# A planner's landing time, 1.9 to 4.0: one constant in the list scheduler of a three-stage kernel

## The chip, the cores and the metric

The kernel runs on one core of one Trainium2 chip. The metric is device time in microseconds of one launch. Engines are named as in the profile: PE (TensorE), DVE (VectorE), ACT (ScalarE), POOL (GpSimd) and SP (SyncE, which issues every transfer here).

## The reference

```python
# attention (b=4, h=8, s=576, d=64): softmax of q over d, of k over the sequence
kv = np.einsum('bhsd,bhse->bhde', softmax_s(k), v)
x = np.einsum('bhsd,bhde->bhse', softmax_d(q), kv)        # then x as 2304 x 512
# first block: w_in 512 x 2048, w_out 2048 x 512
h = x @ w_in
x = (h * np.clip(h + 3.0, 0.0, 6.0) / 6.0) @ w_out
# second block: 4 experts, w1 512 x 1024, w2 1024 x 512, p = domain_probs normalised per token
out = sum(p[:, e:e+1] * (np.maximum(x @ w1[e], 0.0) @ w2[e]) for e in range(4))
```

## The kernel before

**Work and stages.** A prologue turns q and k of the four batches into the first block's input `x0` (`k_part`, `q_part`, `x_part`). A first stage computes the first block, 16 chunks of 128 hidden columns over six token blocks of 384 (`h_part`: products on L638 to L640, then L682). Its weights come in 64-bit form and are rebuilt word by word on DVE, ACT and POOL (`w_part`: load L576, then L586 to L608). Meanwhile other weights for the end are prepared and stored to DRAM (`w_prepare`: ACT L831, POOL, store L837 into `vd`). Then come three units of 768 tokens of the second block. Unit 0 prepares its weights as it goes and stores some (`w_first0`, `w_second0`: load L872, ACT L897 and L931, store L903; PE L1094 and L1216). Units 1 and 2 load what was stored (`w_bring`, L864; PE L973 and L1289). Every value is split in a high and a low part, and three matmuls make one product. POOL's and some of DVE's element-wise work goes through one helper, L347.

**The order of the work.** No engine's order is written by hand. Each piece of work is an `Op` with a cost on each engine that may do it, its dependencies, the buffer it takes and the buffers it gives back. `Plan.order()` runs a model of the core in time: on each engine, when its clock is free, it takes the op with the smallest key among those whose inputs have arrived and whose buffer is free. The ops are then emitted in the order of their modelled starts, so each engine's queue holds that order and runs it first come, first served, waiting on semaphores for what really happens. The modelled times are used for nothing else. The model starts SP at 2.0 (`FIRST`) and the engines at 5.6 (`BEGIN`).

A transfer costs its KB divided by 400 on SP, one after the other (`dma(n)`, 0.64 for 256 KB, 0.72 for 288 KB, 1.28 for 512 KB). What depends on it arrives `LAND` after that:

```python
def hop(a, b):
    return LAND if a == "SP" else HOPS[b]
...
    # in Plan.order():
    o.due = min((x.due - self.after(e, x) for x in o.then), default=1e6) - o.eng[e].lat
...
    for kind, name in o.give:                       # a buffer given back by o
        self.free[kind].append([..., o.end + hop(e, "")])
    for x in o.then:
        x.at = max(x.at, o.end + self.after(e, x))  # when x may start
```

From SP to SP `after` gives 0. An op's key is its due time (worked back from the PE products in their fixed turn) plus a small bias; the first stage's own DVE and ACT work has keys near -10000, so it always goes first; output stores have key 0. PE's products of each stage are chained, so their order among themselves is fixed. Only one kind of buffer is given back by a transfer: the tiles `wr` of `w_prepare`, free once the store L837 has landed (two of them at first, four from a late part of the first stage on).

Of the kernel before, what the change touches and what calls it, by code (L numbers as in the profile page):

```python
# [76 lines left out]


HOPS = {"PE": 0.06, "ACT": 0.05, "DVE": 0.05, "Pool": 0.09, "SP": 0.05, "": 0.0}
LAND = 1.9  # L80


class Cost(float):
# [9 lines left out]
def hop(a, b):  # L93
    return LAND if a == "SP" else HOPS[b]

# [1439 lines left out]
```

## Time and profile before

| what | value |
|---|---|
| median of 3 runs | 1235.85 us (1231.95 to 1236.56) |
| the profiled execution | 1234.68 us, span 1232.9 us |
| PE busy | 1197.6 us (97%), 7296 matmuls |
| DVE, ACT, POOL busy | 779.1, 600.7, 757.7 us |
| mean granted TensorE clock | 0.994 of full speed |
| DMA | 238.99 MB, mean 194 GB/s |
| chain that ended last | PE 80%, POOL 6%, DMA 5%, DVE 4% |

PE's busy time is that of the matmuls as the profile models them. Times in rows are counted from the start of the span. "Issue to landing" is from SP's issue of a transfer to the moment at which its semaphore says that it has landed.

### The profile page before, as it was taken

The page shows a single profiled execution, that of the slowest core. Times are in us where ns is not written, and L with a number is a line of the kernel's source. Part 1 is how long each engine was busy: PE and PEld are TensorE (multiplying, and loading weights), DVE is VectorE, ACT ScalarE, POOL GpSimd, SP SyncE. Part 2 cuts the span into 40 slices and gives each one's busy share as a digit, 9 for nine tenths or more (in the row PEclk, how much of TensorE's full clock was granted, in tenths as well). Part 3 has the DMA queues.
Part 4 walks back from the last instruction along what each step waited for, and adds up shares of the span by engine and source line. Part 5 has one row for each costly group of instructions (what it writes and reads, how often), then busy time and mean ns, then how long its engine had stood idle before and what let it go on. Part 6 is the DMA issues. An engine that isn't in the chain of part 4 may idle for free.

```text
span 1232.9 us, 21178 instructions
## 1 busy us (share of the span) xinstructions
PE 1197.6 (97%) x7296; PEld 1146.5 (93%) x7296; DVE 779.1 (63%) x1362; ACT 600.7 (49%) x1256; POOL 757.7 (61%) x780
## 2 busy tenths in 40 slices
PE   5699999999999999999999999999999999999998
PEld 4589999999999999988988889999999999999998
DVE  6877731668763555555555575666666966666665
ACT  6667544645554543644444444444444544444441
POOL 4677677766688630877777705655555565555552
PEclk9899999999999999999999999999999999999999
DMA  9533444244367430565555547877777787777771
GB/s 318 154 95 104 162 162 164 103 145 147 135 222 256 152 131 1 178 214 180 182 182 190 183 159 232 275 248 250 249 248 250 241 294 250 247 247 249 246 249 59
DMA packets 125275, 238.99 MB, mean 194 GB/s; under 512 B 14064, under 2 KB 14064, under 8 KB 125168
## 3 DMA queue, kind: packets, MB, share of 16 engines
q1 hardware_dynamic: 125168, 237.64, 57.9%
q8 instruction: 58, 0.95, 0.3%
q14 instruction: 49, 0.40, 0.1%
HBM read 174.14 MB, written 63.44 MB: 193 GB/s over the span
## 4 chain that ended last, share of the span: by engine, by line
PE 80%; POOL 6%; DMA 5%; DVE 4%; issue 3%; ACT 1%; SPq 0%; DVEq 0%; POOLq 0%; ACTq 0%
PE ps L1289 19%; PE ps L973 19%; PE ps L1216 11%; PE ps L1094 9%; PE ps L682 9%; POOL w L347 3%; PE ps L638 3%; PE ps L640 3%; PE ps L639 3%; DMA vd<-w 3%; POOL st L347 1%; DMA qs<-in_q_dram 1%; PE ps L437 1%; POOL wtmp L347 1%; PE ps L531 1%
## 5 line engine op out<-in xcount | busy, mean ns | idle before, releaser
L973 PE MATMUL ps<-x,w 128*128 128x384 f32 x1344 | 264.4, 335 | 0.0
L1289 PE MATMUL ps<-w,g 128*128 128x256 f32 x1737 | 244.0, 283 | 1.7 <-DVE acc L1338 1.7
L347 POOL TENSOR_TENSOR w<-st,w 128x256 fp32r<-128x256 f32 (+1 forms) x174 | 173.8, 1016 | 114.7 <-ACT w L931 76.8
L1289 PEld LDWEIGHTS ps<-w,g 128*128 128x128 f32 x1737 | 228.6, 189 | 5.0 <-DVE acc L1338 5.0
L682 PE MATMUL ps<-g,w 128*128 128x384 f32 x1152 | 223.2, 339 | 5.0 <-ACT g L661 4.1
L973 PEld LDWEIGHTS ps<-x,w 128*128 128x128 f32 x1344 | 227.2, 189 | 0.8
L347 POOL TENSOR_TENSOR g<-t,g 128x384 fp32r<-128x384 f32 x128 | 140.9, 1109 | 124.8 <-ACT g L996 108.4
L682 PEld LDWEIGHTS ps<-g,w 128*128 128x128 f32 x1152 | 199.4, 188 | 12.4 <-ACT g L661 7.6
L1338 DVE SCALAR_TENSOR_TENSOR acc<-ps,pt,acc 128x256 f32<-128x256 f32 x312 | 144.2, 480 | 99.2 <-PE ps L1289 97.6
L1216 PE MATMUL ps<-w,g 128*128 128x512 f32 x576 | 148.9, 394 | 0.0
L1094 PE MATMUL ps<-x,w 128*128 128x384 f32 x672 | 131.0, 335 | 0.0
L655 DVE SCALAR_TENSOR_TENSOR r<-r,ps 128x384 f32<-128x384 f32 x96 | 53.0, 552 | 122.1 <-ACT r L652 114.4
L638 PE MATMUL ps<-x,w 128*128 128x384 f32 x384 | 129.0, 336 | 0.0
L640 PE MATMUL ps<-x,w 128*128 128x384 f32 x384 | 128.5, 335 | 0.3 <-POOL w L347 0.3
L639 PE MATMUL ps<-x,w 128*128 128x384 f32 x384 | 128.3, 334 | 0.0
L1094 PEld LDWEIGHTS ps<-x,w 128*128 128x128 f32 x672 | 119.4, 188 | 7.8
L1216 PEld LDWEIGHTS ps<-w,g 128*128 128x128 f32 x576 | 106.6, 188 | 16.7
L347 POOL TENSOR_TENSOR st<-st 128x256 f32<-128x256 f32 (+1 forms) x66 | 74.4, 1131 | 48.6 <-DVE st L601 45.3
L996 ACT ACTIVATE g<-t 128x384 fp32r<-128x384 f32 x143 | 74.6, 525 | 59.3 <-DVE t L1038 21.6
L652 ACT ACTIVATE r<-ps,three 128x384 f32<-128x384 f32 x96 | 55.4, 577 | 76.1 <-PE ps L640 75.0
L347 POOL TENSOR_TENSOR t<-t 128x384 f32<-128x384 f32 x47 | 47.9, 1020 | 45.3 <-ACT t L981 38.9
L981 ACT ACTIVATE t<-ps 128x384 f32<-128x384 f32 x104 | 50.3, 484 | 52.1 <-PE ps L973 51.5
(145 smaller groups left out, 1852.4 us busy)
## 6 DMA issues: line engine op xcount, KB each, us to landing
w<-wd SPq DMA_DIRECT2D x224, 256.0 KB, 3.1
w<-vd SPq DMA_DIRECT2D x224, 256.0 KB, 3.6
vd<-w SPq DMA_DIRECT2D x112, 256.0 KB, 2.2
wd<-w SPq DMA_DIRECT2D x112, 256.0 KB, 3.5
st<-in_w_dram SPq DMA_DIRECT2D x64, 256.0 KB, 3.5
st<-in_w_dram SPq DMA_DIRECT2D x30, 512.0 KB, 3.9
raw<-in_w_dram SPq DMA_DIRECT2D x32, 256.0 KB, 3.7
out_dram<-acc SPq DMA_DIRECT2D x18, 256.0 KB, 2.5
```

The costliest lines, as they stand in the source:

```text
L347: on(o).tensor_tensor(out=out, in0=a, in1=b, op=op)
L638: nc.tensor.matmul(pst[0], lhsT=hi, rhs=a, start=(k == 0), stop=False)
L639: nc.tensor.matmul(pst[0], lhsT=hi, rhs=b, start=False, stop=False)
L640: nc.tensor.matmul(pst[0], lhsT=lo, rhs=a, start=False, stop=(k == NK - 1))
L652: nc.scalar.activation(out=pst["r"], in_=pst[0], func=AF.Relu, bias=three)
L682: nc.tensor.matmul(y, lhsT=l, rhs=r, start=(s["start"] and not low and m == 0), stop=(s["stop"] and bool(low)))
L973: nc.tensor.matmul(bank(i), lhsT=l, rhs=r, start=(opens and k == 0 and m == 0), stop=(k == 1 and m == 2), skip_group_check=not opens)
L996: nc.scalar.activation(out=made[i][0][:, :n], in_=at(src), func=AF.Relu if raw else AF.Copy)
L1094: nc.tensor.matmul(bank(i), lhsT=l, rhs=r, start=(opens and k == 0 and m == 0), stop=(k == 1 and m == 2), skip_group_check=not opens)
L1216: nc.tensor.matmul(y, lhsT=l, rhs=rr, start=opens and x == 0, stop=closes and x == len(seq) - 1)
L1289: nc.tensor.matmul(y, lhsT=l, rhs=r, start=clears and x == 0, stop=x == len(seq) - 1, skip_group_check=True)
L1338: o1 = add({"DVE": dvep(half)}, lambda o: nc.vector.scalar_tensor_tensor(out=a, in0=y, scalar=s, in1=a, op0=ALU.mult, op1=ALU.add), [made])
```

## The change

The model's time from the end of a transfer's stream to its landing goes from 1.9 to 4.0. Nothing that computes is touched. The constant enters three things: when an op that needs a loaded tile may start in the model, when a `wr` tile is free again after its store, and the due time of each transfer and of all that leads to it.

```diff
 HOPS = {"PE": 0.06, "ACT": 0.05, "DVE": 0.05, "Pool": 0.09, "SP": 0.05, "": 0.0}
-LAND = 1.9
+LAND = 4.0
```

## Rows read from the trace of the kernel before

**Rows 1.** Stretch, length, each engine's busy us (instructions), granted clock, DMA share, GB/s.
```profile
0.00:100.00 100.00, 75.97 (x435) 62.54 (x436) 76.26 (x173) 68.00 (x149) 62.96 (x63) 0.93 0.57 184
...
240.00:420.00 180.00, 174.61 (x979) 168.37 (x979) 116.83 (x190) 95.41 (x200) 131.16 (x141) 1.00 0.52 177
...
500.00:980.00 480.00, 480.00 (x2853) 453.56 (x2852) 305.54 (x494) 226.15 (x477) 300.52 (x310) 1.00 0.66 218
980.00:1200.00 220.00, 218.82 (x1546) 217.20 (x1546) 152.32 (x278) 94.79 (x194) 128.43 (x120) 1.00 0.79 254
```

**Rows 2.** PE's waits in 240 to 420: for whom, us, times, longest.
```profile
PE ps L682 <- ACT g L661: 4.1, 7, 1.5
PE ps L640 <- POOL w L347: 0.3, 1, 0.3
```

**Rows 3.** Transfers in the first 26 us: KB each, median us to landing.
```profile
acc<-in_kt_dram SPq DMA_DIRECT2D x6, 288.0 KB, 4.7
...
qs<-in_q_dram SPq DMA_DIRECT2D x6, 256.0 KB, 4.8
```

**Rows 4.** Transfers between 26 and 100 us, the same view.
```profile
st<-in_w_dram SPq DMA_DIRECT2D x5, 512.0 KB, 3.9
acc<-in_kt_dram SPq DMA_DIRECT2D x7, 288.0 KB, 3.1
...
qs<-in_q_dram SPq DMA_DIRECT2D x6, 256.0 KB, 2.9
```

**Rows 5.** Order of time from 0 to 9 us: start, us, instruction, idle before.
```profile
1.19 0.42 SPq L418 DMA_DIRECT2D acc<-in_kt_dram  x1
...
3.38 0.69 DVE L494 TENSOR_REDUCE qm<-qs 128x8 f32<-128x512 f32 x1 [1.96 <-DMA qs<-in_q_dram]
...
5.94 0.69 DVE L494 TENSOR_REDUCE qm<-qs 128x8 f32<-128x512 f32 x1 [1.87 <-DMA qs<-in_q_dram]
6.54 0.74 DVE L449 TENSOR_REDUCE nm<-acc 128x1 f32<-128x576 f32 x1
```

**Rows 6.** The first two transfers: KB, us from issue to landing.
```profile
acc<-in_kt_dram SPq DMA_DIRECT2D x1, 288.0 KB, 3.0
qs<-in_q_dram SPq DMA_DIRECT2D x1, 256.0 KB, 2.6
```

**Rows 7.** Order of time from 26.8 to 32 us, DVE and PE.
```profile
26.92 1.38 PE L437 MATMUL ps<-vs,acc 128*128 128x129 f32 x10 [0.38 <-DVE acc L344]
...
28.79 0.69 DVE L494 TENSOR_REDUCE qm<-qs 128x8 f32<-128x512 f32 x1 [1.92 <-DMA qs<-in_q_dram]
...
30.59 0.16 DVE L444 RECIPROCAL rs<-ps 128x1 f32<-128x1 f32 x1
...
31.29 1.09 PE L430 MATMUL ps<-ident,acc 128*128 128x128 f32 x4 [2.98 <-DVE bd L445]
```

**Rows 8.** The chain that ended last, its piece from 21 to 29 us.
```profile
21.12 7.57 DMA qs<-in_q_dram
```

**Rows 9.** The stretch with the lowest clock, columns as in Rows 1.
```profile
30.00:35.00 5.00, 3.34 (x14) 2.77 (x15) 4.09 (x11) 2.27 (x7) 3.99 (x4) 0.50 0.37 116
```

**Rows 10.** DVE's waits for transfers in the first 120 us: us, times, longest.
```profile
DVE qm L494 <- DMA qs<-in_q_dram: 9.3, 7, 2.0
...
DVE qm L494 <- DMA spare<-in_q_dram: 1.8, 1, 1.8
```

**Rows 11.** SP's longest wait in the first 120 us, the same columns.
```profile
SPq L420 <- PE ps L437: 26.1, 8, 10.1
```

**Rows 12.** ACT's waits in 200 to 420 us, the longest in total.
```profile
ACT w L831 <- DMA vd<-w: 36.2, 35, 4.1
```

**Rows 13.** The stores of line 837 between 140 and 220 us.
```profile
L837 SPq DMA_DIRECT2D vd<-w x37: 319/320/399, 142.1 to 218.8; - x37
...
DMA to landing us min/median/max: 2.0/2.0/3.9
```

**Rows 14.** POOL's longest wait between 400 and 520 us.
```profile
POOL w L347 <- ACT w L931: 52.8, 2, 51.2
```

## The prediction

> **What bounds the kernel now.** I read first the busy time by stretch. From 500 to 980 us PE is busy in all 480 us, and from 980 to 1200 in 218.8 of 220; between 240 and 420 it loses 5.4 us, and in the first 100 us it loses 24.0 [rows 1]. So the kernel is bound by PE's fixed sequence of matmuls, and an order that a planner makes can move only what PE loses: 24.0 in the prologue, 5.4 in the middle of the first stage, little more behind. Next, who PE waited for: in the middle it is mostly ACT (4.1 of the 5.4), and nowhere in that list a transfer [rows 2]. In the prologue DVE is busy 76.3 of 100 us and leads PE [rows 1], and DVE does wait for transfers, 9.3 and 1.8 us [rows 10]. So a landing time matters here through DVE's and ACT's queues, which run in the order that the plan gave them and stand still at an op whose load has not landed.
>
> The constant is a guess about landings, so the third view is what they really take. In the plan a 256 KB load asked for on an idle queue lands 0.64 + 1.9 = 2.54 after its issue, and with the change 4.64; for 288 KB it is 2.62 and 4.72, for 512 KB 3.18 and 5.28. On the chip these loads took 4.8 and 4.7 us while everything was loading at once [rows 3], and 2.9, 3.1 and 3.9 us afterwards [rows 4]. So in the first 26 us 4.0 is the better guess (some of that time is queueing, which the plan counts separately). Behind that both are wrong: 1.9 is 0.4 to 0.7 too early, 4.0 is 1.4 to 1.7 too late.
>
> **Three things that cannot change.** The constant adds no instruction and no byte. PE's products keep their order within a stage, as they are chained. Due times move, but those of all plain loads by the same 2.1, so their order on SP among themselves changes only where the time at which a buffer comes free decides. SP stands waiting for such buffers anyway, 26.1 us for one of them alone [rows 11]; a load that is put ahead of another can block it there, and this is why I keep a slower case.
>
> **The change part by part.**
>
> *The opening.* In the plan before, the first q tile arrives at 4.54, the first k tile at 5.26, the second q at 5.90; DVE starts at 5.6, so when it has reduced the first q (0.6) both others are there and the smaller key wins: q, q, k. The trace shows that order, and that DVE stood idle for 1.87 us before the second q [rows 5], although the first k, issued at 1.19, had landed 3.0 us later, at 4.19 [rows 5, 6]. With 4.0 the arrivals are 6.64, 7.36 and 8.00. DVE is free of the first q at 7.24, and the k tile comes next: q, k, q. On the chip the k reduction (0.74) then fits into the idle 1.87. I take 0.7 us saved; bounds nothing (DVE's total work is the same, and what follows may wait for something else) and 1.9.
>
> *The gap at 28 us.* PE ends a product at 28.30 and then waits 2.98 us for `bd`, which DVE makes on L444 and L445. DVE could not: it waited 1.92 us for a q tile at the head of its queue, then did three other ops, and reached L444 at 30.59 [rows 7]. That q tile was 7.57 us on its way [rows 8]. If the plan lets it arrive 2.1 later, its reduction falls behind ops that were ready, and L444 can start as early as 28.3: 2.3 us sooner. The idle stretch also has a second price. After it the granted clock was 0.50 for 5 us, in which PE was busy 3.34 us [rows 9]; at full clock that is half, 1.7 less. Together 4.0. Other ops may get in front of L444 in the new order as well, so I take 3.0, bounds 0 and 4.0.
>
> *The later loads of the prologue.* The 16 k tiles go through four buffers, so behind the first generation come three more, each with a landing in its chain. There the plan will expect a tile 1.7 us later than it lands (4.64 against 2.9), and puts other work in front of its first op. If all three generations pay this on the path to PE, it is 5.1; with the full 2.1 each, 6.3; if DVE, which is busy three quarters of the time, had other work to do anyway, nothing. I take the middle, 2.6 lost.
>
> *The first stage, stores.* A `wr` tile is free in the plan at 2.54 after its store's start, and then at 4.64. Really stores landed in 2.0 us between 140 and 220 [rows 13], yet ACT waited 36.2 us for them between 200 and 420, up to 4.1 at a time [rows 12], because the stores started late. With the tile planned free 2.1 later, ACT's op L831 stands further back in its queue, and the op of the main chain behind it is not held up. The main chain's waits for ACT are 4.1 us of PE time [rows 2]. Not all come from L831; I take 1.5 saved, bounds 0 and 4.1.
>
> *The same stores, the other way.* The preparation becomes slower. Two tiles in a ring give one store per half cycle; 37 stores took from 142.1 to 218.8, 2.13 us each [rows 13]. With 2.1 more per cycle it is 1.05 more each, 3.18, so in that stretch 24 are done in place of 37. The 13 missing come at the end, where the ring has four tiles and a cycle in the plan of 4.64 + 1.3 (0.3 on ACT, 0.7 on POOL and the hops, by the plan's costs) for four, 1.5 each: 20 us later. This is hidden by POOL's wait of 51.2 us in 400 to 520, in which all of this work is over and there is no buffer to go on with [rows 14]. Cost nothing; if the delay grew past 51 us, PE would stand for what is above it.
>
> *The first stage, the 64-bit weights.* Their load is planned 2.1 later, and DVE's, ACT's and POOL's steps with it. Really a 512 KB load takes 3.9 [rows 4], so they stand 1.4 too late in their queues. PE waited for such a tile once, 0.3 us [rows 2]; two or three chunks are needed at once where the pass over all six blocks begins. Bounds nothing and 3 x 2.1 = 6.3; I take 1.0 lost.
>
> *Units 0 to 2.* PE never lacked a weight tile in 500 to 980 [rows 1]: nothing.
>
> *Sum.* -0.7 - 3.0 + 2.6 - 1.5 + 1.0 = -1.6. Against the profiled execution's own 1234.68 that is 1233.1. The median of the runs lies 1.2 above the profiled one, so against it I forecast 1234. The bounds added up are -10.0 (1.9 + 4.0 + 4.1) and +12.6 (6.3 + 6.3), 1226 and 1248.
>
> A rule of the Trainium skill speaks against the change: "DMA: Bandwidth & Descriptors", section "Anatomy of one DMA", gives a transfer a fixed part of about 2.0 us beside bytes at 436 GB/s, on another issue path than SP's. For 256 KB that makes 2.6 us, and the first transfer, alone on the queue, did take 2.6 [rows 6]. By the rule 1.9 would be right everywhere, the first and second terms would be empty, and the sum would be +2.1; the landings of 4.7 and 4.8 under load [rows 3] say otherwise for the opening.
>
> **The rivals.**
>
> *Faster.* All of DVE's waits for transfers in the prologue but the first, unavoidable one (9.3 + 1.8 - 1.96 = 9.1 [rows 5, 10]) come off PE's path, and with them the slow clock at 30 us (1.7) [rows 9]: -10.8, 1225. For it speaks that they are the wait that the constant aims at; against it that DVE is busy 76.3 of the 100 us, so much of what is filled in returns as work later. Chance 0.25.
>
> *Slower.* A first op on a landed tile, or a load on SP behind one that waits, comes late on the prologue's path. Three generations at 2.1 are 6.3, and if PE thereby gets one more idle stretch like that at 28 us (2.98 idle and 1.7 of slow clock), it is +11.0: 1247. It decides from the point at which an op on a k or q tile starts more than 2 us after its landing while PE is idle. Against it speaks that in the plan all consumers move alike. Chance 0.24.
>
> *The ring of stores.* The preparation ends more than 51 us later than now, PE stands at the start of unit 0; at twice the 20 us worked out it does not. Were it four times, 80 us, PE would lose 29: 1265. Chance 0.05.
>
> *No effect.* The order changes only among ops that do not lead PE: 1236. This and the forecast fall in the same class, together 0.46 (0.36 for the forecast, 0.10 for this).
>
> **How the numbers follow.** About 0.5%, 6 us, is what a measurement of this kernel can tell from no change. Faster than that 0.25, within it 0.36 + 0.10 = 0.46, slower 0.24 + 0.05 = 0.29. The likeliest time is 1234. The range reaches from the faster rival, 1225, with 3 us more for a second gap closed, to the slower one, 1247, with 4 more for the same reason: 1222 to 1251; the ring and extremes of the others lie outside.
>
> **What would show it.** In the new trace: DVE's second reduction is of a k tile; its waits for q tiles in the first 120 us fall below 11 us; no PE wait of 3 us at 28 us; ACT's wait for stores in 200 to 420 well under 36 us; fewer than 30 stores of L837 between 140 and 220, the last of them some 20 us later than now, POOL's 51 us wait shortened by as much; PE full from 500 on. Wrong would be: the prologue's loss above 30 us, new stretches at a clock of 0.5, PE waiting for POOL or DVE on weight tiles between 220 and 300, or PE idle at the start of unit 0.

## The result, and the profile after

The changed kernel takes 1223.5 us (median of 4 runs, 1222.7 to 1224.9) against 1235.5 before: a ratio of 0.9909, 95% interval 0.9887 to 0.9931. It is faster by 0.9%, 12 us. The time lies in the range that I gave, near its lower end; the likeliest case, no change that can be told, did not come. (The median before is that of four runs; the 1235.85 ahead of the prediction was that of the first three.) The profiled execution has a span of 1223.1 us.

Busy time by stretch, after (the columns of [rows 1]):

```profile
0.00:100.00 100.00, 79.47 (x445) 66.07 (x446) 80.56 (x179) 69.07 (x150) 63.31 (x63) 0.90 0.58 192
...
240.00:420.00 180.00, 178.82 (x1031) 178.38 (x1030) 124.67 (x198) 97.86 (x206) 134.43 (x142) 1.00 0.50 172
...
500.00:980.00 480.00, 478.82 (x2855) 451.76 (x2854) 303.08 (x496) 223.57 (x470) 299.13 (x307) 1.00 0.67 218
980.00:1200.00 220.00, 220.00 (x1555) 218.20 (x1554) 150.18 (x274) 93.47 (x192) 126.55 (x119) 1.00 0.78 248
```

The second busy column is that of PE's weight loads, the figure in brackets their number. Between 240 and 420 it goes from 168.37 (979 loads) to 178.38 (1030): 10 us more of full work in the same 180 us. The first busy column, the matmuls', shows only 4.2 of that (174.61 to 178.82). Behind 500 the weight loads differ by less than 2 us in either stretch.

The start of PE's products on line 638 gives the same account as a clock (four such matmuls belong to one step of the first stage, of which there are 96). Undisturbed, a step takes 4.16 us. Step 12, behind the prologue's thick part, starts at 137.9 us before and 136.6 after; step 36 at 237.7 and 236.5; unit 0's first matmul (L1094) at 500.1 and 489.8; from there to the start of the last matmul it is 728.4 and 728.9. So in these two profiles 1.3 us come from the prologue, 9.1 from the first stage behind step 36, and none from the units. (What the prologue's share is worth in other executions is told below.)

What stood in PE's way in that stretch has gone. PE's weight loads show the wait for ACT in full; between 240 and 420, first before, then after (us, times, longest):

```profile
PEld ps L682 <- ACT g L661: 7.6, 11, 1.8
```

```profile
PEld ps L682 <- ACT g L661: 1.5, 1, 1.5
```

The matmuls' only wait for ACT there, after, in us, times and longest (4.1 in 7 before [rows 2]), and ACT's wait for stores between 200 and 420 (36.2 us in 35 before [rows 12]):

```profile
PE ps L682 <- ACT g L661: 1.2, 1, 1.2
```

```profile
ACT w L831 <- DMA vd<-w: 1.7, 1, 1.7
```

The prologue, after: rows of the first 7 us in order of time, and DVE's only wait for loads in the first 120 (9.3 and 1.8 before [rows 10]):

```profile
3.43 0.69 DVE L494 TENSOR_REDUCE qm<-qs 128x8 f32<-128x512 f32 x1 [2.02 <-DMA qs<-in_q_dram]
4.21 0.75 DVE L449 TENSOR_REDUCE nm<-acc 128x1 f32<-128x576 f32 x1
...
5.92 1.30 PE L430 MATMUL ps<-ident,acc 128*128 128x128 f32 x5 [5.92 <-ACT acc L451]
6.13 0.69 DVE L494 TENSOR_REDUCE qm<-qs 128x8 f32<-128x512 f32 x1 [1.17 <-DMA qs<-in_q_dram]
```

```profile
DVE qm L494 <- DMA qs<-in_q_dram: 3.2, 2, 2.0
```

DVE takes a k tile second, where the q tile stood [rows 5], and PE's first transposes start at 5.92; before it was 8.24 (PE's first wait there is 8.2 us long). The 3 us gap at 28 us [rows 7] is gone as well; the wait for `bd` near there is 1.18 us now. But the slow clock is not. Stretches of 5 us, columns as in [rows 9]:

```profile
30.00:35.00 5.00, 3.45 (x18) 2.56 (x18) 4.40 (x12) 2.94 (x9) 2.46 (x3) 0.65 0.56 137
35.00:40.00 5.00, 3.79 (x16) 3.06 (x16) 4.34 (x9) 2.32 (x6) 5.00 (x4) 0.50 0.79 278
40.00:45.00 5.00, 5.00 (x19) 4.76 (x19) 3.60 (x10) 3.36 (x7) 2.48 (x4) 0.50 0.80 247
```

Before, the clock was 0.50 in one such stretch, from 30 to 35, and 0.84 in the next; here it is 0.65, 0.50 and 0.50. (A second slow stretch, from 60 to 65, is there in both: 0.55 and 0.50.) New stretches at 0.5 were among the prediction's signs of being wrong. PE's longest wait behind 30 us has grown as well, from 3.32 to 4.85, at 61 us, for DVE's `x` (L531). Both stand against the shorter waits for loads; how much of the gain each took is not shown.

The preparation's stores, after, between 140 and 220 [rows 13], and POOL's longest wait in 400 to 520 [rows 14]:

```profile
L837 SPq DMA_DIRECT2D vd<-w x25: 319/320/330, 141.8 to 219.7; - x25
...
DMA to landing us min/median/max: 2.0/2.0/3.9
```

```profile
POOL w L347 <- ACT w L931: 23.4, 2, 21.8
```

25 stores in place of 37. The last is at 455.7 in place of 412.4, and POOL's wait has shrunk from 51.2 to 21.8. PE pays nothing for it: between 420 and 500 its weight loads are busy 79.9 us before and after.

### The profile page after: what moved, and what is told of

Its sections match the earlier page's. It is cut to its first block, busy times and chain, and to the rows that moved or that the text cites. A ratio compares the mean times of both kernels' runs of the same rounds, so it can differ in the third digit from the quotient of the medians.

```text
span 1223.1 us, 21176 instructions
## 1 busy us (share of the span) xinstructions
PE 1195.6 (98%) x7296; PEld 1149.7 (94%) x7296; DVE 780.9 (64%) x1364; ACT 597.1 (49%) x1253; POOL 762.3 (62%) x781
## 4 chain that ended last, share of the span: by engine, by line
PE 95%; DVE 3%; ACT 1%; issue 1%; DMA 0%; DVEq 0%; SPq 0%; ACTq 0%
PE ps L1289 20%; PE ps L973 19%; PE ps L682 16%; PE ps L1216 11%; PE ps L1094 10%; PE ps L639 5%; PE ps L640 5%; PE ps L638 5%; PE ps L531 1%; PE ps L437 1%; PE ps L430 1%; PE ps L492 1%; DVE st L592 0%; DVE acc L1338 0%; DVE nm L449 0%
## 5 line engine op out<-in xcount | busy, mean ns | idle before, releaser
L973 PEld LDWEIGHTS ps<-x,w 128*128 128x128 f32 x1344 | 227.2, 189 | 0.8
L347 POOL TENSOR_TENSOR g<-t,g 128x384 fp32r<-128x384 f32 x131 | 144.2, 1112 | 125.7 <-ACT g L996 109.2
L682 PE MATMUL ps<-g,w 128*128 128x384 f32 x1152 | 220.7, 337 | 1.2 <-ACT g L661 1.2
L1094 PE MATMUL ps<-x,w 128*128 128x384 f32 x672 | 131.0, 335 | 0.0
L1094 PEld LDWEIGHTS ps<-x,w 128*128 128x128 f32 x672 | 119.4, 188 | 7.8
L996 ACT ACTIVATE g<-t 128x384 fp32r<-128x384 f32 x160 | 82.8, 524 | 79.4 <-DVE t L1060 36.3
L638 PEld LDWEIGHTS ps<-x,w 128*128 128x128 f32 x384 | 72.7, 189 | 0.3
L639 PEld LDWEIGHTS ps<-x,w 128*128 128x128 f32 x384 | 72.5, 189 | 0.3
```

The source lines that it names most:

```text
L347: on(o).tensor_tensor(out=out, in0=a, in1=b, op=op)
L638: nc.tensor.matmul(pst[0], lhsT=hi, rhs=a, start=(k == 0), stop=False)
L639: nc.tensor.matmul(pst[0], lhsT=hi, rhs=b, start=False, stop=False)
L682: nc.tensor.matmul(y, lhsT=l, rhs=r, start=(s["start"] and not low and m == 0), stop=(s["stop"] and bool(low)))
L973: nc.tensor.matmul(bank(i), lhsT=l, rhs=r, start=(opens and k == 0 and m == 0), stop=(k == 1 and m == 2), skip_group_check=not opens)
L996: nc.scalar.activation(out=made[i][0][:, :n], in_=at(src), func=AF.Relu if raw else AF.Copy)
```

## The experiments

**How the loss comes about.** One of the losses, followed back in the trace of the kernel before. Order of time from 246 to 268 us, several engines, rows of other work left out:

```profile
246.97 2.01 SPq L576 DMA_DIRECT2D st<-in_w_dram  x2
250.47 0.91 DVE L586 TENSOR_SCALAR st<-st 128x512 int32<-128x512 int32 x1 [3.02 <-DMA st<-in_w_dram]
253.32 0.43 DVE L586 TENSOR_SCALAR st<-st 128x512 int32<-128x512 int32 x1 [1.94 <-DMA st<-in_w_dram]
256.95 0.68 DVE L601 SCALAR_TENSOR_TENSOR st<-st 128x512 f32<-128x512 uint32 x1
257.71 1.65 POOL L347 TENSOR_TENSOR st<-st 128x512 f32<-128x512 f32 x1 [4.33 <-DVE st L601]
259.32 0.74 POOL L347 TENSOR_TENSOR w<-wtmp,w 128x256 fp32r<-128x256 f32 x1
259.39 0.33 SPq L576 DMA_DIRECT2D st<-in_w_dram  x1
...
260.09 3.60 SPq L837 DMA_DIRECT2D vd<-w  x2
265.15 0.42 ACT L831 ACTIVATE w<-wtmp 128x256 fp32r<-128x256 f32 x1 [3.94 <-DMA vd<-w]
...
266.04 0.51 ACT L661 ACTIVATE g<-r 128x384 fp32r<-128x384 f32 x1
266.60 1.53 PEld L682 LDWEIGHTS ps<-g,w 128*128 128x128 f32 x9 [0.42 <-ACT g L661]
```

Read downwards: DVE stands 3.02 and 1.94 us for two 512 KB loads; POOL, first come first served, stands 4.33 for DVE's result; a `w` tile behind that is ready only at 260.06, so the first of the two stores goes out at 260.09, 0.70 behind another 512 KB load. It lands 5.0 us after its issue, where the plan has 2.54; ACT stands 3.94 us for it; the main chain's L661 stands behind ACT's op, and PE's weight loads for the next products stand 0.42 us and start at 266.60.

This store is no exception. Landings of all 73 stores of L837 between 240 and 420, before:

```profile
DMA to landing us min/median/max: 2.0/2.3/5.7
```

ACT's longest wait, 4.13 us at 291, is for the one that took 5.7. Both kinds of landing, load and store, are in this chain, and I began with two theories that take one each, A (stores) and B (64-bit weight loads), beside C (any reshuffle).

The two kernels and the twelve runs in one table. Loss: 180 us less the busy weight loads between 240 and 420. The waits are those of ACT for stores (L831) and of DVE for loads (L586) in the same stretch. Step 12: its start, from the same profile. Times are medians, ratios those to the kernel before on the same chip.

| kernel | loss | ACT's wait | DVE's wait | step 12 | us | ratio (95%) |
|---|---|---|---|---|---|---|
| before, LAND 1.9 | 11.6 | 33.2 | 8.8 | 137.9 | 1235.5 | |
| changed, 4.0 | 1.6 | 1.7 | 0 | 136.6 | 1223.5 | 0.9909 (0.9887 to 0.9931) |
| 1: stores alone 4.0 | 3.8 | 2.7 | 4.3 | 141.3 | 1229.5 | 0.9949 (0.9932 to 0.9966) |
| 2: loads alone 4.0 | 3.0 | 26.7 | 0 | 134.7 | 1224.0 | 0.9911 (0.9896 to 0.9926) |
| 3: 64-bit loads alone 4.0 | 4.7 | 19.5 | 0 | 141.7 | 1229.8 | 0.9962 (0.9947 to 0.9977) |
| 4: 1.9, three wr tiles | 7.2 | 11.1 | 9.2 | 139.5 | 1233.3 | 0.9990 (0.9977 to 1.0003) |
| 5: 1.9, hops of ACT, DVE 0.06 | 6.5 | 22.8 | 2.6 | 132.9 | 1226.1 | 0.9925 (0.9905 to 0.9946) |
| 6: k, q, v loads alone 4.0 | 5.0 | 22.2 | 2.0 | 131.5 | 1222.2 | 0.9897 (0.9879 to 0.9915) |
| 7: LAND 1.0 | 18.1 | 30.2 | 6.6 | 144.7 | 1257.9 | 1.0186 (1.0163 to 1.0209) |
| 8: LAND 2.9 | 2.7 | 4.8 | 0 | 131.4 | 1220.5 | 0.9883 (0.9868 to 0.9898) |
| 9: 1.9, hop of POOL 0.10 | 5.4 | 21.4 | 6.8 | 138.6 | 1230.7 | 0.9967 (0.9956 to 0.9977) |
| 10: 1.9, hop of PE 0.07 | 8.5 | 23.7 | 8.2 | 138.6 | 1233.9 | 0.9992 (0.9978 to 1.0006) |
| 11: 4.0, hops of ACT, DVE 0.06 | 2.1 | 0 | 0.2 | 136.3 | 1223.4 | 0.9897 (0.9874 to 0.9920) |
| 12: LAND 6.0 | 2.7 | 0 | 0 | 132.8 | 1231.2 | 0.9969 (0.9954 to 0.9984) |

**1. Only the stores.**

```diff
-LAND = 1.9
+LAND, FREE = 1.9, 4.0
...
-    self.free[kind].append([..., o.end + hop(e, "")])
+    self.free[kind].append([..., o.end + (FREE if e == "SP" else hop(e, ""))])
```

> LAND stays 1.9 for every load; only the time at which a wr tile comes free after its store L837 is 4.0. Theory A (the stores): the 9 us that the changed kernel gained between steps 42 and 75 of the first stage come from ACT no longer standing at L831 for a store that has not landed. It expects 1226 to 1228 us (-8 to -10), ACT's wait for stores in 240 to 420 under 5 us (33.2 before), PE's weight loads busy at least 177 of the 180 us there. Theory B (the 64-bit weight loads): the gain comes from DVE no longer standing at L586 for a 512 KB load (8.8 us before). It expects 1233 to 1238 here, with ACT's wait changed or not. Theory C (any reshuffle of the order moves the time by some us): no relation between ACT's wait and the time.

**2. Only the loads** (the same lines with `LAND, FREE = 4.0, 1.9`).

> The other half: 4.0 for all that waits for a load, 1.9 for the wr tiles. Theory A: ACT's wait for stores stays 25 us or more, stage 1 loses 9 us or more of PE's weight loads in 240 to 420, the time is 1232 to 1236 (the prologue's 1.3 us alone). Theory B: 1225 to 1228, DVE's wait at L586 near nothing. Theory C: anywhere from 1222 to 1245.

ACT's waits with us, times and longest, and the stretch of 240 to 420, first with the stores alone, then with the loads alone:

```profile
ACT w L831 <- DMA vd<-w: 2.7, 6, 0.7
```

```profile
240.00:420.00 180.00, 178.30 (x1021) 176.24 (x1020) 120.82 (x195) 96.22 (x201) 130.64 (x138) 1.00 0.49 170
```

```profile
ACT w L831 <- DMA vd<-w: 26.7, 25, 3.0
```

```profile
240.00:420.00 180.00, 178.82 (x1025) 177.05 (x1024) 122.05 (x194) 99.18 (x206) 132.99 (x143) 1.00 0.52 180
```

A falls: with the loads alone ACT still waits 26.7 us for stores, and PE loses 3.0 us, not 9. B falls as well: the stores alone, with DVE's wait halved only, take the loss from 11.6 to 3.8. Each half does most of it, and the halves don't add. In time, run 1 lies between A's numbers and B's: its step 12 starts 3.4 us later than before.

**3. Only the 64-bit weights' loads** (`dma(512, 4.0)`, where `dma` takes the landing time of one transfer).

> 4.0 only for the 512 KB loads of the 64-bit weights (L576); everything else at 1.9. Theory A: 1233 to 1238, ACT's wait for stores 25 us or more. Theory B: 1226 to 1229. Theory C: anywhere from 1222 to 1245.

The loss is 4.7, so B's own load is enough to cut it by 7; the time misses B's numbers by 1 us only. But C's fit all three runs by now.

**4. More time without a planned landing: three wr tiles.**

```diff
-MORE_W, MORE_G, MORE_T = 2, 4, 3
+MORE_W, MORE_G, MORE_T = 3, 4, 3
```

> LAND back at 1.9, but three wr tiles in place of two from the end of the prologue (five in place of four later), so that a tile has more time to land before its turn. The plan will use the third tile to go faster, up to the rate of POOL. Theory A: ACT's wait for stores falls below 20 us of 33.2 and PE gets back at least 4 us, 1226 to 1232. Theory B: 1233 to 1238, whatever ACT's wait is. Theory C: no relation.

ACT's wait falls to 11.1 as A said and the loss to 7.2, but 100 to 240 now loses (weight loads 135.1 of 140 us, 137.7 before), while 47 stores are made between 140 and 220 in place of 37; that these cause it is not shown. The time is the same within its interval: a miss for A's 1226 to 1232 (B's 1233 to 1238 holds, but B had fallen with run 1). The plan used the third tile to go faster and not to wait less.

**5 and 6. Two edits that leave the first stage's landings alone.** My theory was now D: the chain above needs both links, and either, planned later, cuts it. The first edit is a control, the second puts `4.0` on the loads of k, q and v alone.

```diff
-HOPS = {"PE": 0.06, "ACT": 0.05, "DVE": 0.05, ...
+HOPS = {"PE": 0.06, "ACT": 0.06, "DVE": 0.06, ...
```

> A control: LAND 1.9, but the hop to ACT and to DVE is 0.06 in place of 0.05, a change that has nothing to do with landings and still reshuffles the order. Theory D (late loads hold up DVE at L586, that delays POOL and the store L837, ACT then stands at L831 for the store with the main chain's L661 behind it; planning either landing later cuts it, so the parts overlap and do not add): both landings are planned as before, so the first stage's loss between 240 and 420, as 180 us less the busy weight loads, stays 9 to 14 us (11.6 before), and the time is 1232 to 1240. Theory C (any other order is better than this unlucky one): the loss falls to 3 to 7 us, as with every edit so far, and the time moves by some us.

> 4.0 only for the loads of k, q and v, which are over at 110 us; the first stage's two landings stay at 1.9. Theory D: the first stage's loss in 240 to 420 stays 9 to 14 us; only the prologue moves, by -4 to +2, 1231 to 1238. Theory C: the loss falls to 3 to 7 us here too, 1225 to 1233.

D's numbers fall in both: the loss is 6.5 and 5.0, where it said 9 to 14. A hundredth of a microsecond in a hop that has nothing to do with a transfer gives 0.75%. The order before was worse than its neighbours, and part of what the change gained, any other order would have gained. Run 6 is as fast as the changed kernel, 1222.2, below C's numbers too, with the first stage's landings still at 1.9: its step 12 starts 6.4 us earlier than before.

**7 and 8. Other landing times.**

> The other way: LAND 1.0, so every tile and every wr is planned 0.9 earlier than before and about 2 earlier than it lands. Theory D: the loss of 240 to 420 rises to 13 us or more, ACT's wait for stores and DVE's at L586 rise above 33 and 9 us, 1237 to 1250. Theory C: the loss falls to 3 to 7 us.

> LAND 2.9, near to what loads take behind the prologue. Theory D: the loss of 240 to 420 lies between 1.6 and 11.6, nearer to 1.6 (3 to 6), DVE's wait at L586 under 5; 1224 to 1231. Theory C: 3 to 7 as well, no order between 1.0, 1.9, 2.9 and 4.0.

The stretch of 240 to 420, with 1.0 and then with 2.9:

```profile
240.00:420.00 180.00, 170.60 (x937) 161.92 (x936) 118.17 (x184) 93.43 (x193) 128.72 (x136) 0.99 0.48 163
```

```profile
240.00:420.00 180.00, 178.06 (x1023) 177.32 (x1024) 115.97 (x191) 99.11 (x211) 138.41 (x152) 1.00 0.55 187
```

Here C falls: with 1.0 the loss is 18.1 and the kernel 1.9% slower, further off than any reshuffle went. D's numbers are missed too: ACT's and DVE's waits for landings, 30.2 and 6.6, are below those of the kernel before, so these two sums alone don't order the runs. With 2.9 the loss is 2.7 and the time the shortest of all, 1220.5, both a little under D's numbers. (2.9 counts from the end of the modelled stream: a 256 KB load then lands 3.54 us after its issue in the plan, a 512 KB load 4.18; measured were 2.9 and 3.9 [rows 4].) That 2.9 is better than 4.0 isn't shown: the intervals of the ratios overlap, the loss is no smaller, and the difference sits in the prologue (step 12 at 131.4 and 136.6), which scatters, as told below.

**9 to 12. How much is the landing, how much the draw?** Two more controls at 1.9 (`"Pool": 0.10`; `"PE": 0.07`), the first control's edit on top of 4.0, and 6.0.

> A second control at LAND 1.9: POOL's hop 0.10 in place of 0.09. Theory C2 (the order before was one unlucky draw among orders that are all alike from 1.9 on): 1222 to 1229, the loss of weight loads in 240 to 420 3 to 7 us, as for the first control. Theory D2 (planned landings set the level of the first stage's loss, the draw adds a few us of scatter to it and to the prologue): 1224 to 1240, the loss 5 to 14, ACT's wait for stores still above 18 us.

> A third control at LAND 1.9: PE's hop 0.07 in place of 0.06. The same numbers as for the second: C2 1222 to 1229 and a loss of 3 to 7; D2 1224 to 1240, the loss 5 to 14, ACT's wait for stores above 18 us. If all three controls stay under 7, D2's share of the gain is small.

> The first control's edit (hops of ACT and DVE 0.06) on top of LAND 4.0. D2: the loss in 240 to 420 stays at 4 us or less, ACT's wait for stores under 5, 1218 to 1228. C2: the loss is drawn anew from 3 to 7, the time from 1222 to 1229, no different from the controls at 1.9.

> LAND 6.0, two us more pessimistic again. D2: the first stage's loss in 240 to 420 stays at 4 us or less, as nothing in it waits for a landing any more; the prologue, whose loads are then planned 3 us later than they land, is 2 to 8 us longer than at 2.9: 1222 to 1232. C2: 1222 to 1229, loss 3 to 7. A preparation that ends more than 51 us later would show as PE standing at the start of unit 0.

The five orders in which the first stage's landings are planned at 1.9 lose 11.6, 6.5, 5.0, 5.4 and 8.5, a mean of 7.4; the two at 4.0 lose 1.6 and 2.1, and 2.9 and 6.0 both 2.7. So D2 holds, the theory that the planned landing sets the level and the order drawn adds some us to it; C2, that all orders from 1.9 on are alike, misses run 10's loss, 8.5, and run 11's, 2.1. Of the 10.0 us that the change gained in this stretch I put 5.6 down to the landing (7.4 less 1.8) and 4.2 to the order before being that much worse than the mean at 1.9 (11.6 less 7.4): estimates from five and two draws. Through which waits the landing sets the level is shown at one place only, in the chain above.

The prologue goes the same way. With its loads planned at 2.9 or more (the changed kernel, runs 2, 6, 8, 11, 12) step 12 starts between 131.4 and 136.6, a mean of 133.9; with 1.9 (the kernel before, runs 1, 3, 4, 5, 9, 10) between 132.9 and 141.7, a mean of 138.6. And in whole times, the four orders with 1.9 everywhere and two `wr` tiles (before, 5, 9, 10) have a mean of 1231.6, the two with 4.0 everywhere 1223.5: by this estimate 8 of the 12 us are the landing and 4 the draw.

With 6.0 the stage itself is as good as at 2.9, the prologue 1.4 us longer (D2 said 2 to 8), and the kernel 11 us slower. PE's wait between 420 and 530, the stretch of 420 to 500, and the stores:

```profile
PE ps L1094 <- DVE x L347: 5.9, 1, 5.9
```

```profile
420.00:500.00 80.00, 73.53 (x407) 72.89 (x406) 43.67 (x67) 39.66 (x88) 51.11 (x66) 0.96 0.50 180
```

```profile
L837 SPq DMA_DIRECT2D vd<-w x112: 319/320/914, 138.0 to 490.0; - x112
```

The last store is at 490.0, unit 0's input forms take their buffers from the preparation, and PE stands 5.9 us for them; behind that, from 495 to 500, the granted clock is 0.50 with PE busy throughout. From L1094 to the last matmul it takes 737.3 us, 8.9 longer than before. This is the rival that I called the ring of stores, at a landing of 6.0 in place of 4.0.

## Why the prediction was right and wrong

**The place.** That only the prologue and the middle of the first stage could move was right: the units take 728.4 and 728.9 us.

**The step that failed: "the first stage, stores", and "the 64-bit weights" beside it.** I gave them 1.5 saved (bounds 0 and 4.1) and 1.0 lost (bounds 0 and 6.3); together they are 9.1 saved, the order before being a bad draw included. The size was wrong because I took PE's loss from the matmuls' busy time, 5.4 of 180 us, and from PE's listed waits, 4.1, and made that the bound. The weight loads in the same row [rows 1] say 168.37 of 180, a loss of 11.6, and their waits for ACT are 7.6, not 4.1. The Trainium skill, in "Trainium Kernel Development and Optimization", section "Performance Expectations", says of how close a kernel is to the roofline that matmul busy time is a bad metric, as matmuls are pipelined, and the weight loads' busy share a good one. For time gained the trace agrees: 4.2 us by the one, 10.0 by the other, for 9.1 measured by the step starts.

The reason that I gave for ACT's waits was wrong as well, that stores land in 2.0 us and only started late. That was read between 140 and 220; where PE loses, stores took up to 5.7, and ACT's longest waits are for these.

The sign of the second term was wrong too, as far as run 3 shows: with the later loads alone the loss falls from 11.6 to 4.7, though two orders with these loads at 1.9 (runs 6 and 9) come near that. I saw that the loads would be planned 1.4 later than they land, and not that with 1.9 DVE stood 8.8 us for them (which is in the waits of that stretch) and that POOL and the store hang on DVE. In the loss followed above a wait for a load and a wait for a store were one chain, and I priced them as two.

And I did not ask how good the order before is among its like: the controls say that some 4 us of the gain are that.

**The opening and the gap at 28 us** came as worked out: k second, PE's first transposes 2.3 us earlier, no 3 us gap. Their sum with the later loads was -1.1, the profiles show -1.3. But that closeness is partly luck. In runs 1 and 4 every engine has the order of the kernel before up to 140 us, and step 12 starts at 141.3 and 139.5 there against 137.9; run 2 has the changed kernel's order to 144 us and starts it at 134.7 against 136.6. So one order's prologue scatters by 2 to 3.5 us, and the mean difference of the two orders is 3.9 (139.6 less 135.7). I also let the slow clock go for 1.7; it came all the same, and for longer: 0.66 on the mean from 30 to 50 us, 0.84 before.

**The ring of stores.** 24 stores worked out for 140 to 220, 25 measured. The end of the preparation is 43 us later, not 20: I had let it catch up at 1.5 us per store, but 57 stores from 341.4 to 455.7 took 2.0 each. It was hidden, as I said; of POOL's 51.2 us, 21.8 were left, so the cover that I counted on is more than half gone, and with 6.0 it is.

**The rivals.** "Faster" came, by 12 us where it said 10.8, but for the most part through ACT's queue in the first stage, not through DVE's waits in the prologue that I built it on. So that the time lies in the range is partly luck: its lower end was made from another mechanism. "Slower", a consumer placed late on the prologue's path, is not seen: with 4.0 for these loads (the changed kernel, runs 2, 6, 11) step 12 starts at 136.6, 134.7, 131.5 and 136.3, and at 137.9 before. By the rule of the Trainium skill that the prediction draws on ("DMA: Bandwidth & Descriptors", section "Anatomy of one DMA"), 1.9 would have been right everywhere. Here it was not: 2.9 and 4.0 are both better, and in the first stage stores of 256 KB took up to 5.7 us, where the rule, which is for another issue path than SP's, gives 2.6 by estimate.

## What to carry to other kernels

A planned latency that is too short makes queues that run in order stand at their heads, and what stands behind can be the main chain; one that is too long cost only slack here, until with 6.0 the slack was used up. Take the planned value from the trace, from issue to landing in the stretch where the time is lost, and look at the long landings there as well as at the median: here 2.9 and 4.0 beat 1.0, 1.9 and 6.0. Before a gain of a per cent from a planner's constant is believed, change another constant by a hair and see what the draw alone does (0.1 to 0.75% here); and take PE's loss from its weight loads or the starts of like steps, not from busy matmuls.

## What the runs showed that I had not expected

The same instruction order up to step 12 took 137.9, 139.5 and 141.3 us in three profiles, while from step 12 to 36 every step of the kernel before took 4.16 us to the hundredth: the prologue scatters by itself, with no change of order. What the rest of one order scatters by is not shown, as it was profiled once. And stores of 256 KB landed 2.0 us after their issue between 140 and 220 (minimum and median of 37 [rows 13]), where loads of 256 KB took 2.9 [rows 4]; between 240 and 420 the median was 2.3, and the longest 5.7.
